# Weight conversion with both halves per instruction and an add of whole words on VectorE, bonus sums of six chunks by TensorE, and a new hand-written first order

## The chip, the cores and the metric

The kernel runs on one core of one Trainium2 chip. The metric is the device time of one execution in microseconds (us). In what follows PE is TensorE, DVE is VectorE, ACT is ScalarE, POOL is GpSimd and SP is SyncE; PEld is PE's weight load. "L156" is line 156 of the kernel before; in the changed kernel the same statements stand some lines later.

## The reference

A linear attention with a decay per channel over 768 steps, for 4 batches and 8 heads of 48 channels, then a feed-forward network (FFN) whose gate is h cos h. Everything is float32.

```python
for t in range(S):                                   # attention, S = 768
    kt, vt, rt, wt = k[:, :, t], v[:, :, t], r[:, :, t], w[:, :, t]
    cur = np.einsum('bhd,bhe->bhde', u[None] * kt, vt)
    y[:, :, t] = np.einsum('bhd,bhde->bhe', rt, state + cur)
    state = wt[:, :, :, None] * state + np.einsum('bhd,bhe->bhde', kt, vt)
x = y as (3072 tokens, 384)
h = x @ w_in                                         # 384 x 2048
out = (h * np.cos(h)) @ w_out                        # 2048 x 384
```

The term with u is the bonus of the present step: for each token and head the sum over the 48 channels of r k u, times v. The kernel calls this sum cd: 128 tokens by 8 heads.

## The kernel before

**Tiling.** The attention is cut into 24 chunks of 128 tokens (4 batches of 6 chunks), taken in the order of the list `order`, two batches side by side. The FFN takes blocks of two chunks (256 tokens). The FFN's 2048 columns are 16 tiles of 128, called f-tiles; two f-tiles make a unit, so a block has 8 units. A unit is `mm1` (18 matmuls into the tile ph, L342), then the gate on ACT, DVE and POOL (L315 to L328), then `mm2` (12 matmuls into acc, L356). Matmuls keep float32 accuracy by splitting each operand into a high part and a rest, and by three products (`PASSES`).

**Weights.** The weights come to the chip as float64 bit patterns, 64 bits a value. An f-tile has two halves ("kinds"): 384 columns of the first matrix and 384 of the second. `fetch_weights` (event `f`) loads one f-tile of raw words, 768 KB, on SP's queue. `load_weights` (event `w`) turns it into float32 and splits it: ACT scales the high word into h and takes the carry rd from the low word (L125), DVE shifts h left by 3 (L155) and puts the sign in (L156), an integer add of h and rd follows (L158, on POOL), ACT casts the high part (L130) and DVE or POOL subtracts to get the rest (L133). With `MERGE = 0` each of these instructions works on one half, 384 words; the rest of the first half is DVE's, that of the second is POOL's (`wlo0="v"`, `wlo1="p"`).

**A chunk** passes these events: `load` (r, k and w with channels on the partitions: tile tt, 674 KB), `lr` (r and k with tokens on the partitions: tile rk), `lv` (v), `decay` (two scans on DVE, L190 and L197, and the products L201 and L202), `diag` (the bonus sums cd, L206 to L209, and two diagonal fills on POOL, L213), `a` (scores pa, L233, and masked copies on DVE, L235), `t` and `s` (state), `d` (decay of the state), `y` (output, L285 and L289, a copy yf on ACT and six small DMAs into xf), `x` (split of xf into xT for the FFN). `NEEDS` and `FREES` list which event must come before which.

**What sets the order.** For the first six chunks and the first two blocks the order is written out by hand: `START` is a list of events, and `PAIR` says for each of the 16 units in it whether it belongs to block 0 or 1. PE follows this order as written. The other engines' queues are ordered by a scheduler that looks at the same events. In this first part the table `EARLY` says which engine does what (v DVE, a ACT, p POOL, s SP); after it `LATER` and the repeating `PLAN` hold, and the weights are done. `BUFS` gives the number of buffers of each tile. All loads and the DMAs into xf stand in one queue, SP's.

```python
        place = min(range(max(f + 1, NF + 1 - RING), NF + 1), key=lambda p: last.get(p, -1))
        nc.gpsimd.tensor_tensor(out=h, in0=h, in1=rd, op=ALU.add)
        nc.vector.copy_predicated(a["asb", h], mask, pa[h])
```

The first line is the place of the raw words: they lie where later weights will stand, in a ring of five. The second is the add on POOL. The third waits for the diagonal fill of the same chunk.

Of the kernel before, what the change touches and what calls it, by code (L numbers as in the profile page):

```python
# [62 lines left out]
@with_exitstack  # L63
def rwkv_cos_ffn(ctx: ExitStack, tc: tile.TileContext, tr, tn, u, wts, w, rkw, vst, us, xs, out):
    nc = tc.nc
# [76 lines left out]
    def load_weights(f):  # L142

        bits = raw.pop(f)
        wgt[f] = wt.tile([128, 2, 2, DM], F32R, tag=f"w{f}", name=f"w{f}")
        step = 2 if MERGE else 1
        for kind in range(0, 2, step):
            high, rest = wgt[f][:, kind:kind + step, 0], wgt[f][:, kind:kind + step, 1]
            words = bits[:, kind:kind + step].rearrange("p k (n w) -> p k n w", w=2)
# [5 lines left out]
            nc.vector.tensor_scalar(out=h, in0=h, scalar1=3, scalar2=None, op0=ALU.logical_shift_left)  # L155
            nc.vector.scalar_tensor_tensor(out=h, in0=hi, scalar=sign_bit, in1=h,  # L156
                                           op0=ALU.bitwise_and, op1=ALU.bitwise_or)
            nc.gpsimd.tensor_tensor(out=h, in0=h, in1=rd, op=ALU.add)  # L158
# [45 lines left out]
    def att_diag(a):  # L204
        rk = a["rk"][:, 0]
        E["rk"].tensor_tensor(out=rk, in0=rk, in1=a["rk"][:, 1], op=ALU.mult)  # L206
        E["ru"].tensor_tensor(out=rk, in0=rk, in1=u_sb, op=ALU.mult)
        cd = buf("cd", [C, 8], F32)
        nc.vector.tensor_reduce(out=cd, in_=rk.rearrange("p (h d) -> p h d", d=HD), axis=mybir.AxisListType.X, op=ALU.add)  # L209
# [403 lines left out]
```

## Time and profile before

| | us |
|---|---|
| median of 3 runs | 604.78 |
| lowest, highest | 603.35, 605.7 |
| the profiled execution | 603.12 |
| its span in the trace | 601.4 |
| PE busy in the span | 524.5 (87%) |
| DVE, ACT, POOL busy | 446.1, 245.2, 268.2 |

The page slices the span into 40 equal parts; each digit is the busy share of a slice in tenths, and in the row PEclk the clock that was granted to PE.

```profile
PE   2513744998998999999999999999999999999995
DVE  6989899998765785786696758858957865767641
ACT  2533765552333334334433353343343334334541
POOL 4675658663333543443354433434434333422231
PEclk9999858897997999999999999999999999999998
```

A slice is 15 us. The hand-written first order takes the first twelve; in the first seven of them PE has low digits and DVE high ones. From the fourteenth on PE is at 9 until the last slice.

### The profile page before, as it was taken

To read this page: it belongs to the slowest core of one execution; us is meant where nothing else is said; L and a number is where in the kernel's file an instruction comes from. 1 tells how busy PE (TensorE), PEld (TensorE's weight loads), DVE (VectorE), ACT (ScalarE), POOL (GpSimd) and SP (SyncE) were. 2 spreads that over 40 slices of the span, in tenths; PEclk is the share of its full clock that TensorE was granted. 3 is DMA by queue.
4 is the path that set the end of the run, shared out by engine and by line. 5 is a ranking of instruction groups with operands and counts; after the bars stand their busy time and mean duration, and the time that the engine had idled before them with its cause. 6 is when DMAs were issued, how large, how long until landed. Compare 5 with 4: busy or idle time off the path is not lost.

```text
span 601.4 us, 11254 instructions
## 1 busy us (share of the span) xinstructions
PE 524.5 (87%) x4372; PEld 496.4 (83%) x4372; DVE 446.1 (74%) x759; ACT 245.2 (41%) x440; POOL 268.2 (45%) x320
## 2 busy tenths in 40 slices
PE   2513744998998999999999999999999999999995
PEld 1403744887988999999999999999999999899994
DVE  6989899998765785786696758858957865767641
ACT  2533765552333334334433353343343334334541
POOL 4675658663333543443354433434434333422231
PEclk9999858897997999999999999999999999999998
DMA  8718156030342134124223121331242032055000
GB/s 267 270 66 320 47 204 191 1 106 27 99 130 78 45 99 122 44 60 126 83 74 116 54 73 53 99 101 47 79 126 65 9 100 73 2 174 187 36 1 32
DMA packets 23725, 58.47 MB, mean 97 GB/s; under 512 B 4208, under 2 KB 15088, under 8 KB 23664
## 3 DMA queue, kind: packets, MB, share of 16 engines
q1 hardware_dynamic: 23664, 57.68, 31.1%
q8 instruction: 36, 0.59, 0.4%
q14 instruction: 25, 0.20, 0.1%
HBM read 48.22 MB, written 4.72 MB: 88 GB/s over the span
## 4 chain that ended last, share of the span: by engine, by line
PE 66%; DVE 19%; DMA 6%; issue 4%; POOL 3%; ACT 1%; SPq 0%; DVEq 0%; POOLq 0%
PE ph L342 29%; PE acc L356 26%; DMA tt<-tr 6%; PE py L285 3%; PE py L289 3%; PE pa L233 3%; POOL h L158 2%; DVE h L156 2%; DVE h L155 2%; DVE shrink L193 2%; PE pst L260 2%; DVE xT L133 2%; DVE rr L320 1%; DVE w L133 1%; PE pt L242 1%
## 5 line engine op out<-in xcount | busy, mean ns | idle before, releaser
L342 PE MATMUL ph<-xT,w 128*128 128x256 f32 x1728 | 226.2, 288 | 36.3 <-DVE xT L130 31.2
L342 PEld LDWEIGHTS ph<-xT,w 128*128 128x128 f32 x1728 | 217.4, 195 | 41.7 <-DVE xT L130 29.4
L356 PE MATMUL acc<-w,gs 128*128 128x384 f32 x1152 | 218.7, 340 | 0.0
L133 POOL TENSOR_TENSOR gs<-rr,gs 128x256 fp32r<-128x256 f32 x176 | 137.7, 801 | 168.5 <-DVE gs L130 152.9
L356 PEld LDWEIGHTS acc<-w,gs 128*128 128x128 f32 x1152 | 197.8, 189 | 2.9 <-issue 0.6
L321 ACT ACTIVATE rr<-rr 128x512 f32<-128x512 f32 x96 | 60.7, 632 | 164.0 <-DVE rr L320 163.9
L319 ACT ACTIVATE rr<-ph 128x512 int32<-128x512 f32 x96 | 57.0, 594 | 102.5 <-PE ph L342 100.0
L323 DVE SCALAR_TENSOR_TENSOR rr<-rr,ph 128x512 f32<-128x512 f32 x96 | 65.4, 681 | 42.5 <-ACT rr L322 42.3
L320 DVE SCALAR_TENSOR_TENSOR rr<-rr,ph 128x512 f32<-128x512 int32 x96 | 65.0, 678 | 33.7 <-ACT rr L319 33.7
L322 ACT ACTIVATE rr<-rr 128x512 f32<-128x512 f32 x96 | 60.6, 631 | 2.5
L158 POOL TENSOR_TENSOR h<-h,rd 128x384 int32<-128x384 int32 x32 | 41.2, 1293 | 22.9 <-DVE h L156 20.1
L190 DVE TENSOR_TENSOR_SCAN ee<-tt,one_e 112x516 f32<-112x516 f32 x24 | 30.8, 1283 | 27.7 <-DMA tt<-tr 27.6
L130 DVE CAST gs<-rr 128x512 fp32r<-128x512 f32 x96 | 41.6, 433 | 6.9 <-PE acc L356 6.8
L213 POOL TENSOR_SCALAR_AFFINE_SELECT asb<-cd 128x512 f32<-128x512 f32 x48 | 32.6, 703 | 19.4 <-PE py L285 13.6
L233 PE MATMUL pa<-tt 48*128 48x128 f32 x384 | 34.1, 310 | 8.0 <-ACT kn L130 3.8
L233 PEld LDWEIGHTS pa<-tt 48*128 48x128 f32 x384 | 28.1, 208 | 14.8 <-ACT kn L130 4.3
L201 POOL TENSOR_TENSOR tt<-tt 112x512 f32<-112x512 f32 x18 | 21.5, 1193 | 35.3 <-DVE tt L197 35.3
L226 POOL TENSOR_TENSOR dd<-sn,ee 112x192 f32<-112x192 f32 x16 | 9.6, 601 | 61.9 <-DVE ee L190 52.1
L130 ACT CAST w<-h 128x384 fp32r<-128x384 f32 x32 | 16.4, 512 | 47.9 <-POOL h L158 47.8
L235 DVE COPY_PREDICATED asb<-mask,pa 128x512 f32<-128x512 uint8 x48 | 32.5, 725 | 0.0
L285 PE MATMUL py<-asb,v 128*48 128x128 f32 (+1 forms) x384 | 30.1, 294 | 1.1 <-DVE asb L235 1.1
L197 DVE TENSOR_TENSOR_SCAN tt<-tt,inj 112x516 f32<-112x516 f32 x24 | 30.8, 1285 | 0.2
(61 smaller groups left out, 428.9 us busy)
## 6 DMA issues: line engine op xcount, KB each, us to landing
tt<-tr SPq DMA_DIRECT2D x24, 674.2 KB, 5.3
raw<-wts SPq DMA_DIRECT2D x16, 768.0 KB, 8.1
rk<-tn SPq DMA_DIRECT2D x24, 384.0 KB, 3.5
v<-tn SPq DMA_DIRECT2D x24, 192.0 KB, 2.4
out<-ob SPq DMA_DIRECT2D x24, 192.0 KB, 2.1
ww<-w SPq DMA_DIRECT2D x6, 768.0 KB, 4.5
xf<-yf SPq DMA_DIRECT2D x48, 72.0 KB, 3.3
xf<-yf SPq DMA_DIRECT2D x48, 16.0 KB, 2.8
```

The source lines that it names most:

```text
L130: (nc.scalar.copy if E[name] is nc.scalar else E[name].tensor_copy)(out=out, in_=in_)
L133: E[name].tensor_tensor(out=out, in0=full, in1=high.bitcast(F32), op=ALU.subtract)
L158: nc.gpsimd.tensor_tensor(out=h, in0=h, in1=rd, op=ALU.add)
L233: nc.tensor.matmul(out=pa[h][:, p], lhsT=a["k3"][rows(h), p], rhs=a["r3"][rows(h), p], start=True, stop=True)
L285: nc.tensor.matmul(out=py[ROW * h:ROW * h + m, p], lhsT=a["v"][:, head_cols(p, h)], rhs=a["asb", h][:, p], start=p == 0, stop=not past, sk ...
L319: nc.scalar.activation(nn, ph, AF.Copy, scale=INV2PI / W_SCALE)
L320: nc.vector.scalar_tensor_tensor(out=rr, in0=nn, scalar=-2.0 * math.pi * W_SCALE, in1=ph, op0=ALU.mult, op1=ALU.add)
L321: nc.scalar.activation(rr, rr, AF.Sin, scale=0.5 / W_SCALE)
L322: nc.scalar.activation(rr, rr, AF.Square)
L323: nc.vector.scalar_tensor_tensor(out=rr, in0=rr, scalar=-0.5, in1=ph, op0=ALU.add, op1=ALU.mult)
L342: nc.tensor.matmul(out=ph[:, fi], lhsT=wgt[u * FU + fi][:, 0, a, kt * 128:(kt + 1) * 128], rhs=xT[:, b, kt], start=n == 0, stop=n == 3 * K ...
L356: nc.tensor.matmul(out=accs[i][j][:, :DM], lhsT=gs[:, a, fi, j * C:(j + 1) * C], rhs=wgt[u * FU + fi][:, 1, b], start=u == 0 and fi == 0 a ...
```

## The change

- **Both halves per instruction.** `MERGE = 1`: every instruction of `load_weights` takes 768 words in place of 384, half as many instructions. The buffers follow: h from 6 of 384 words to 2 of 768, rd from 3 to 1.
- **The add on DVE.** `wadd="v"`: the integer add of h and rd is DVE's, not POOL's. Since the second half has no instruction of its own any more, `wlo1="p"` is without effect and the whole rest (768) is DVE's too. POOL has no part in the conversion any more. (A second way of setting the sign is in the code, with the tiles sign and three; with `wsg="v"` it isn't used.)
- **Bonus sums by PE for chunks 0 to 5** (`BY_PE = 6`). `decay` begins with a product rkt = r k on DVE, channels on the partitions; four small matmuls against u laid out by head (`u_by_head`, a new load of 112x8 values) sum it into pc, and ACT copies pc to cd. These six chunks load no rk; the load of u_sb moves behind the load of chunk 6.
- **Buffers:** tt 2 to 3, v 2 to 4.
- **A new `START` and `PAIR`.** `lr0` to `lr5` are gone, the units and the conversions stand otherwise to each other. Before, the 16 conversions were done ahead of the 14th `mm1`; now the last two stand between the 14th and the 15th.

```diff
-MERGE = 0
-BUFS = dict(tt=2, rk=2, v=2, h=6, rd=3, rr=7, ... cd=1)
+MERGE = 1
+BUFS = dict(tt=3, rk=2, v=4, h=2, rd=1, sign=1, rr=7, ... cd=1, rkt=1)
...
+         "y2 f w f load4 y3 s3 f w t3 mm1 mm2 mm2 decay4 w load5 mm1 load6 w mm1 decay5 diag4 lv4 lr6 f f t4",
...
-PAIR = "0000110111110001"
+PAIR = "0000111011101001"
@@ load_weights
-            scaled("wm", h.bitcast(F32), hi.bitcast(F32), 2.0 ** -111)
+            nc.scalar.activation(h.bitcast(F32), hi.bitcast(F32), AF.Copy, scale=2.0 ** -111)
             rd = buf("rd", [128, step, DM], I32)
-            scaled("rd%d" % kind, rd, lo.bitcast(U32), 2.0 ** -29)
+            nc.scalar.activation(rd, lo.bitcast(U32), AF.Copy, scale=2.0 ** -29)
...
-            nc.gpsimd.tensor_tensor(out=h, in0=h, in1=rd, op=ALU.add)
+            E["wadd"].tensor_tensor(out=h, in0=h, in1=rd, op=ALU.add)
@@ att_load
+        if j == 0:
+            E["qt"].dma_start(out=u_by_head, in_=ut)
+        if j == BY_PE:
+            E["qt"].dma_start(out=u_sb, in_=u.to_broadcast([C, DM]))
@@ att_decay
+        if a["j"] < BY_PE:
+            a["rkt"] = buf("rkt", [R, NP, C], F32)
+            E["rkt"].tensor_tensor(out=a["rkt"], in0=a["r3"], in1=a["k3"], op=ALU.mult)
@@ att_diag
+        if a["j"] < BY_PE:
+            pc = bank("a", [C, 512], "pc")[:, :8]
+            for p in range(NP):
+                nc.tensor.matmul(out=pc[:, 2 * p:2 * p + 2], lhsT=a["rkt"][:, p], rhs=u_by_head[:, p], start=True, stop=True)
+            cd = buf("cd", [C, 8], F32)
+            copy("cd", cd, pc)
+        else:
...
```

What this does to the queues is seen at three places. **DVE, the first f-tile and the second chunk's scans, before** (w_161 is the first f-tile):

```order
L156 SCALAR_TENSOR_TENSOR h<-raw,sign_bit,h 128x384
L190 SCALAR_TENSOR_TENSOR ee<-tt,one_e 112x516
L155 TENSOR_SCALAR h<-h 128x384
L193 TENSOR_TENSOR shrink<-shrink,ee 112x4
L195 TENSOR_SCALAR whole<-ee 112x4
L156 SCALAR_TENSOR_TENSOR h<-raw,sign_bit,h 128x384
L196 RECIPROCAL inj<-whole 112x4
L235 COPY_PREDICATED asb<-mask,pa 128x512
L197 SCALAR_TENSOR_TENSOR tt<-tt,inj 112x516
L235 COPY_PREDICATED asb<-mask,pa 128x512
L201 TENSOR_TENSOR tt<-tt 112x512
L133 TENSOR_TENSOR w_161<-h,w_161 128x384
```

and now, where the first f-tile is called w_178 (the row ISA is the integer add, over 1536 elements of 16 bits):

```order
L160 SCALAR_TENSOR_TENSOR h<-raw,sign_bit,h 128x768
L201 TENSOR_TENSOR rkt<-tt 112x512
L204 SCALAR_TENSOR_TENSOR ee<-tt,one_e 112x516
L167 ISA h<-h,rd 128x1536
L207 TENSOR_TENSOR shrink<-shrink,ee 112x4
L209 TENSOR_SCALAR whole<-ee 112x4
L210 RECIPROCAL inj<-whole 112x4
L211 SCALAR_TENSOR_TENSOR tt<-tt,inj 112x516
L256 COPY_PREDICATED asb<-mask,pa 128x512
L215 TENSOR_TENSOR tt<-tt 112x512
L256 COPY_PREDICATED asb<-mask,pa 128x512
L136 TENSOR_TENSOR w_178<-h,w_178 128x2x384
```

The add and the whole rest of the tile have come to DVE, in place of two instructions per step there is one, and the product rkt stands ahead of the scan.

**ACT, from the second chunk's kn to its output copy yf, before** (w_296 and w_379 are the third and fourth f-tile):

```order
L130 COPY kn<-pt 128x384
L125 ACTIVATE h<-raw 128x384
L130 CAST w_296<-h 128x384
L125 ACTIVATE rd<-raw 128x384
L125 ACTIVATE h<-raw 128x384
L130 CAST w_296<-h 128x384
L125 ACTIVATE rd<-raw 128x384
L125 ACTIVATE h<-raw 128x384
L130 CAST w_379<-h 128x384
L125 ACTIVATE rd<-raw 128x384
L130 CAST w_379<-h 128x384
L130 COPY yf<-py 112x512
```

and now (w_314 is the third f-tile):

```order
L133 COPY kn<-pt 128x384
L155 ACTIVATE h<-raw 128x768
L133 CAST w_314<-h 128x2x384
L133 COPY yf<-py 112x512
L157 ACTIVATE rd<-raw 128x768
L155 ACTIVATE h<-raw 128x768
L133 CAST w_324<-h 128x2x384
```

The copy yf of chunk 1 stood behind both casts of the fourth f-tile; now it stands behind the third's, and the rd of the next f-tile comes after the cast of this one.

**POOL, from the first diagonal fill, before:**

```order
L213 AFFINE_SELECT asb<-cd 128x512 x2
L158 TENSOR_TENSOR h<-h,rd 128x384
L202 TENSOR_TENSOR tt<-tt,ee 112x512
L158 TENSOR_TENSOR h<-h,rd 128x384
L133 TENSOR_TENSOR w_161<-h,w_161 128x384
L158 TENSOR_TENSOR h<-h,rd 128x384
L213 AFFINE_SELECT asb<-cd 128x512 x2
```

and now:

```order
L234 AFFINE_SELECT asb<-cd 128x512 x3
L216 TENSOR_TENSOR tt<-tt,ee 112x512
L234 AFFINE_SELECT asb<-cd 128x512 x2
L216 TENSOR_TENSOR tt<-tt,ee 112x512
L234 AFFINE_SELECT asb<-cd 128x512
L216 TENSOR_TENSOR tt<-tt,ee 112x512
L136 TENSOR_TENSOR gs<-rr,gs 128x256
```

Between the fills and the products of the decay nothing is left of the conversion.

More of the change, by code (lines that the diff above doesn't have):

```diff
@@ L27 @@
 BLK = 2
+BY_PE = 6
 BT = BLK * C
@@ L31 @@
 BY_HAND = "P"
-MERGE = 0
-BUFS = dict(tt=2, rk=2, v=2, h=6, rd=3, rr=7, gs=2, asb=4, ahl=2, sn=2, yf=1, past=2, xT=2, kn=2, ee=2, dd=2, xf=6, cd=1)
+MERGE = 1
+BUFS = dict(tt=3, rk=2, v=4, h=2, rd=1, sign=1, rr=7, gs=2, asb=4, ahl=2, sn=2, yf=1, past=2, xT=2, kn=2, ee=2, dd=2, xf=6, cd=1, rkt=1)
 LEAST = 1e-15
@@ L63, in rwkv_cos_ffn @@
 @with_exitstack
-def rwkv_cos_ffn(ctx: ExitStack, tc: tile.TileContext, tr, tn, u, wts, w, rkw, vst, us, xs, out):
+def rwkv_cos_ffn(ctx: ExitStack, tc: tile.TileContext, tr, tn, u, ut, wts, w, rkw, vst, us, xs, out):
     nc = tc.nc
@@ L107, in rwkv_cos_ffn @@
     u_sb = cst.tile([C, DM], F32, name="u_sb")
+    u_by_head = cst.tile([R, NP, 2], F32, name="u_by_head")
     shrink = cst.tile([R, NP], F32, name="shrink")
@@ L115, in rwkv_cos_ffn @@
     nc.vector.memset(sign_bit, -(1 << 31))
+    three = cst.tile([128, 1], I32, name="three")
+    nc.vector.memset(three, 3)
     raw, wgt, last = {}, {}, {}
@@ L151, in load_weights @@
             h = buf("h", [128, step, DM], I32)
-            scaled("wm", h.bitcast(F32), hi.bitcast(F32), 2.0 ** -111)
+            nc.scalar.activation(h.bitcast(F32), hi.bitcast(F32), AF.Copy, scale=2.0 ** -111)
             rd = buf("rd", [128, step, DM], I32)
-            scaled("rd%d" % kind, rd, lo.bitcast(U32), 2.0 ** -29)
[L155 to L158, printed above, removed]
+            nc.scalar.activation(rd, lo.bitcast(U32), AF.Copy, scale=2.0 ** -29)
+            if E["wsg"] is nc.vector:
+                nc.vector.tensor_scalar(out=h, in0=h, scalar1=3, scalar2=None, op0=ALU.logical_shift_left)
+                nc.vector.scalar_tensor_tensor(out=h, in0=hi, scalar=sign_bit, in1=h,
+                                               op0=ALU.bitwise_and, op1=ALU.bitwise_or)
+            else:
+                sign = buf("sign", [128, step, DM], I32)
+                nc.gpsimd.tensor_scalar(out=sign, in0=hi, scalar1=-(1 << 31), scalar2=None, op0=ALU.bitwise_and)
+                nc.vector.scalar_tensor_tensor(out=h, in0=h, scalar=three, in1=sign,
+                                               op0=ALU.logical_shift_left, op1=ALU.bitwise_or)
+            E["wadd"].tensor_tensor(out=h, in0=h, in1=rd, op=ALU.add)
             hf = h.bitcast(F32)
@@ L178, in att_load_rk @@
         E["qr"].dma_start(out=rk, in_=tn[a["g"], :, 0:2])
-        if a["j"] == 0:
-            E["qr"].dma_start(out=u_sb, in_=u.to_broadcast([C, DM]))
     def att_load_v(a):
@@ L204, in att_diag @@
     def att_diag(a):
[L205 to L209, printed above, removed]
+        if a["j"] < BY_PE:
[4 more added lines that the diff above has]
+            copy("cd", cd, pc)
+        else:
+            rk = a["rk"][:, 0]
+            E["rk"].tensor_tensor(out=rk, in0=rk, in1=a["rk"][:, 1], op=ALU.mult)
+            E["ru"].tensor_tensor(out=rk, in0=rk, in1=u_sb, op=ALU.mult)
+            cd = buf("cd", [C, 8], F32)
+            nc.vector.tensor_reduce(out=cd, in_=rk.rearrange("p (h d) -> p h d", d=HD), axis=mybir.AxisListType.X, op=ALU.add)
         for h in range(2):
@@ L386, in att @@
             return
-        for m in NEEDS.get(n, "").split():
+        for m in ("decay" if n == "diag" and j < BY_PE else NEEDS.get(n, "")).split():
             att(j, m)
@@ L592, in slay @@
         return x.reshape(B, NP, 2, S, D).transpose(3, 2, 4, 0, 1).reshape(S, 2 * D, B * NP)
+    ut = np.zeros((2, ROW, NP, 2), np.float32)
+    for h in range(2):
+        ut[h, :D, :, h] = u.reshape(NP, 2, D)[:, h].T
     us = np.broadcast_to(u.reshape(NP, 2, D).transpose(1, 2, 0).reshape(2 * D, 1, NP), (2 * D, B, NP))
```

5 lines of the change are left out of this document (3 added, 2 removed), and 8 rows, old and new, of the table START.

## Prediction

> **What bounds the kernel now.** I read first the busy time by stage, cut where the program changes: the first FFN matmul (53.5 us), the last FFN matmul of the hand-written first order (177.4), the tail (570, left out here). Columns: window, length, then busy time and count of PE, PEld, DVE, ACT, POOL, granted clock, DMA share, GB/s.
>
> ```profile
> 0.00:53.50 53.50, 13.55 (x104) 10.80 (x104) 45.17 (x76) 19.50 (x40) 31.39 (x33) 1.00 0.63 208
> 53.50:177.40 123.90, 98.69 (x754) 92.72 (x755) 107.77 (x182) 62.04 (x121) 67.87 (x63) 0.86 0.35 115
> 177.40:570.00 392.60, 388.13 (x3352) 369.06 (x3351) 283.93 (x486) 154.13 (x264) 160.28 (x213) 0.99 0.28 83
> ```
>
> From 177.4 us on PE is busy 388.1 of 392.6 us and the change leaves that code alone. PE stands idle 40.0 + 25.2 = 65.2 us in the first order; that is the only place where this change can win or lose. There DVE is busy 45.2 + 107.8 = 152.9 of 177.4 us, the most of the four engines that feed PE. So the first order is set by the length of DVE's queue and by its idle 24.5 us, and the rest of the program follows its end one for one.
>
> Next, what DVE does in 0 to 177.4 us (groups by line and shape: total us, mean ns of one):
>
> ```profile
> L156 DVE SCALAR_TENSOR_TENSOR h<-raw,sign_bit,h 128x384 int32<-128x384 int32 x32 | 26.4, 832 | 0.1
> L155 DVE TENSOR_SCALAR h<-h 128x384 int32<-128x384 int32 x32 | 17.9, 581 | 0.8 <-ACT h L125 0.8
> L133 DVE TENSOR_TENSOR w<-h,w 128x384 fp32r<-128x384 f32 x16 | 10.9, 687 | 4.6 <-ACT w L130 4.6
> L190 DVE TENSOR_TENSOR_SCAN ee<-tt,one_e 112x516 f32<-112x516 f32 x8 | 10.9, 1360 | 8.2 <-DMA tt<-tr 8.1
> L133 DVE TENSOR_TENSOR gs<-rr,gs 128x256 fp32r<-128x256 f32 x16 | 9.8, 614 | 0.1
> L130 DVE CAST gs<-rr 128x512 fp32r<-128x512 f32 x16 | 8.4, 522 | 1.1 <-PE acc L356 1.1
> L207 DVE TENSOR_TENSOR rk<-rk,u_sb 128x384 f32<-128x384 f32 x10 | 6.3, 628 | 0.0
> L206 DVE TENSOR_TENSOR rk<-rk 128x384 f32<-128x384 f32 x10 | 6.0, 605 | 0.0
> L133 DVE TENSOR_TENSOR xT<-xf,xT 128x384 fp32r<-128x384 f32 x5 | 6.0, 1191 | 0.0
> L209 DVE TENSOR_REDUCE cd<-rk 128x8 f32<-128x384 f32 x9 | 4.9, 544 | 1.6 <-POOL asb L213 1.6
> L193 DVE TENSOR_TENSOR shrink<-shrink,ee 112x4 f32<-112x4 f32 x7 | 4.5, 643 | 0.1
> L226 DVE TENSOR_TENSOR dd<-sn,ee 112x192 f32<-112x192 f32 x4 | 4.0, 1002 | 0.0
> L158 POOL TENSOR_TENSOR h<-h,rd 128x384 int32<-128x384 int32 x32 | 41.2, 1293 | 22.9 <-DVE h L156 20.1 <-ACT w L130 1.1 <-ACT rr L321 1.1
> L133 POOL TENSOR_TENSOR w<-h,w 128x384 fp32r<-128x384 f32 x16 | 18.9, 1184 | 7.5 <-ACT w L130 7.5
> ```
>
> A multiply of 4 elements (L193) that takes 643 ns on average is the thing to notice. The timeline shows why, and gives each form's undisturbed time:
>
> ```profile
> 5.55 1.23 DVE L190 TENSOR_TENSOR_SCAN ee<-tt,one_e 112x516 f32<-112x516 f32 x1 [3.48 <-DMA tt<-tr]
> 22.26 0.34 DVE L155 TENSOR_SCALAR h<-h 128x384 int32<-128x384 int32 x1
> 28.19 0.61 DVE L156 SCALAR_TENSOR_TENSOR h<-raw,sign_bit,h 128x384 int32<-128x384 int32 x1
> 32.23 1.18 POOL L202 TENSOR_TENSOR tt<-tt,ee 112x512 f32<-112x512 f32 x1 [1.49 <-PE py L285]
> 32.26 1.16 DVE L193 TENSOR_TENSOR shrink<-shrink,ee 112x4 f32<-112x4 f32 x1
> 33.42 0.55 DVE L133 TENSOR_TENSOR w<-h,w 128x384 fp32r<-128x384 f32 x1
> 34.63 3.56 POOL L158 TENSOR_TENSOR h<-h,rd 128x384 int32<-128x384 int32 x1 [1.23 <-DVE h L156]
> 36.13 0.68 DVE L201 TENSOR_TENSOR tt<-tt 112x512 f32<-112x512 f32 x1
> 63.56 0.42 DVE L130 CAST gs<-rr 128x512 fp32r<-128x512 f32 x1
> 173.71 0.42 DVE L133 TENSOR_TENSOR gs<-rr,gs 128x256 fp32r<-128x256 f32 x1
> 178.12 0.17 DVE L193 TENSOR_TENSOR shrink<-shrink,ee 112x4 f32<-112x4 f32 x1
> ```
>
> The L193 at 32.26 us ran until a POOL instruction that began 0.03 us before it was over (1.16 against 1.18 us); the one at 178.12 took 0.17. And a POOL add beside a busy DVE took 3.56 us. **DVE and POOL hold each other up**, so work taken from POOL is partly won on DVE.
>
> **The change part by part.**
>
> *Weights, both halves per instruction.* On DVE today: 26.4 + 17.9 + 10.9 = 55.2 us. At the undisturbed times it would be 32 x 0.61 + 32 x 0.34 + 16 x 0.55 = 39.2, so 16.0 us are waits for POOL. Afterwards a tile is four instructions over 768 words. From 0.55 us (384, two inputs) and 0.68 (512, two inputs) 384 words more cost 0.39: low part 0.94, sign 1.00; the shift, 0.34 with one input, gets half of that, 0.53. The add is new on DVE and the trace of before has none like it. The order shows it as one instruction over 1536 16-bit elements. By bytes it is a two-input instruction over 768 words, 0.94 us; by elements it is 0.55 + 1152 x 0.13/128 = 1.72. I take 0.94, because the two-input rows differ by the bytes they carry, and keep 1.72 for the range. Sum 3.41 x 16 = 54.6 us undisturbed, as much as the disturbed 55.2 of today although DVE takes over 32 adds and 16 low parts.
>
> [...]
>
> *POOL.* It loses L158 and its half of the low parts, 41.2 + 18.9 = 60.1 of the 31.4 + 67.9 = 99.3 us in the first order; 0.39 is left. I scale the waits on DVE by that. Of the weights' 16.0 us 6.3 stay: weights 54.6 + 6.3 = 60.9, **+5.7 us**. In the other rows the waits are: gs (614 - 420) x 16 = 3.1, xT (1191 - 550) x 5 = 3.2, L193 (643 - 170) x 7 = 3.3, the gate's casts (522 - 420) x 16 = 1.6, L190 (1360 - 1230) x 8 = 1.0, and L226, half as long as a 0.55 us row, at least (1002 - 550) x 4 = 1.8. Of these 14.0 us 0.61 goes: **-8.5 us**.
>
> *Bonus sums by PE.* Six chunks lose L206, L207, L209: 6 x (0.605 + 0.628 + 0.544) = 10.7 us, and gain a product of 112x512 (L201's form, 0.68): 4.1. **-6.6 us**. For the 24 small matmuls there are two rows of PE:
>
> ```profile
> 29.14 0.98 PE L260 MATMUL pst<-v,kn 128*64 128x48 f32 x15 [0.87 <-ACT kn L130]
> L242 PE MATMUL pt<-ident,tt 112*128 112x112 f32 x26 | 5.0, 327 | 12.5 <-POOL tt L202 8.1 <-DVE asb L235 4.4
> ```
>
> They cost PE between 24 x 0.98/15 = 1.6 us (the state matmuls' pace) and 24 x 0.327 = 7.8 (a transpose each); I take 2, the nearer in size, and count nothing, for they lie in PE's 65 us of idle time; without that cover they would be the 2. The six cd copies go to ACT, busy 81.5 of 177.4 us; each is a new wait, for behind a late copy stand the two diagonal fills on POOL, then the masked copies on DVE and the output matmuls on PE. POOL's queue, freed of the conversion, leaves them room, so I count nothing; a whole ACT cast late each time it would be 6 x 0.76 = 4.6.
>
> *Idle time of DVE.* The row that matters is on the way to the first FFN matmul:
>
> ```profile
> ACT w L130 <- POOL h L158: 47.8, 27, 6.1
> ACT h L125 <- DMA raw<-wts: 8.7, 1, 8.7
> 38.23 0.51 ACT L130 CAST w<-h 128x384 fp32r<-128x384 f32 x1 [6.06 <-POOL h L158]
> 42.18 0.58 ACT L130 COPY yf<-py 112x512 f32<-112x512 f32 x1
> 53.57 0.58 PE L342 MATMUL ph<-xT,w 128*128 128x256 f32 x1 [21.60 <-DVE xT L130]
> ```
>
> PE had finished chunk 1's output at 53.57 - 21.60 = 32.0 us, but its copy (42.18) stood on ACT behind a cast that waited 6.06 us for the slow POOL add; 11.4 us after the copy PE could start. Now that copy stands behind the third tile's cast, which follows the third add on DVE. By the order and the times above DVE's rows up to that add come to 24 us; with 3.5 us until the first chunk lands, some 5 us of waits and ACT's cast and copy it is at about 35 us instead of 42. And the first raw weights (ACT waited 8.7 us) have no rk and no u_sb in front of them on SP; six rk loads go, u_sb moves behind the load of chunk 6, and a load of 3.6 KB comes. I expect the first FFN matmul some 7 us earlier, and of the 20 us of DVE's idle time after the first chunk's arrival 4 us gone; bounds 12 gone and, with shallower h and rd buffers, 28 more (below). **-4 us**.
>
> *New first order, PAIR, tt and v buffers.* The order moves weights 15 and 16 behind more FFN units and puts chunk 1's product ahead of chunk 0's scores on PE, so these wait for the second tt load. DVE's queue is no shorter for that: 0, bounds as for the idle time. After the first order nothing is left to win, as the third stretch of the first view shows.
>
> Sum: 5.7 - 8.5 - 6.6 - 4 = **-13.4 us**. The profiled run took 603.1 us (its span 601.4 and 1.7 around it), so 589.7; the median of the runs, 604.8, lies 1.7 us above that run and gives 591.4. I say 591.
>
> **The rivals.**
>
> *PE becomes the bound of the first order (more gained).* If the chains shorten more, 12 instead of 4 us of DVE's idle time go: 583; if the waits for POOL go altogether too (6.3 us and 5.5 that I left standing), 572. For it: ACT's 47.8 us behind POOL vanish. Against: DVE's own rows stay, and PE needs its 16 + 16 units after its first FFN matmul whatever comes, which is 67 us by the chain in order of time (18 matmuls 2.12 us, 12 matmuls 2.09):
>
> ```profile
> 215.53 2.12 PE ph L342 x18
> 217.65 2.09 PE acc L356 x12
> ```
>
> Chance 0.2, around 581.
>
> *The add runs an element a tick.* 16 x (1.72 - 0.94) = 12.5 us more on DVE: 604, no measurable change. For it: no row shows two inputs at two elements a tick. Chance 0.12.
>
> *One rd buffer makes a ring (slower).* Before, rd had three buffers and h six halves; now ACT may write the next tile's rd only after DVE's add has read this one, and in ACT's queue that stands behind this tile's cast. Cast and rd have the rows
>
> ```profile
> L125 ACT ACTIVATE rd<-raw 128x384 int32<-128x384 uint32 x32 | 17.4, 545 | 0.0
> L321 ACT ACTIVATE rr<-rr 128x512 f32<-128x512 f32 x16 | 10.1, 629 | 15.5 <-DVE rr L320 15.4
> ```
>
> so 128 words more cost ACT 0.084 us; over 768 words the cast (0.51 at 384) takes 0.76 and rd 0.80, and with hand-overs the ring is some 1.75 us. If DVE sits through that on every tile it loses 16 x 1.75 = 28 us: 619. It makes the kernel slower from (13.4 + 3) / 16 = 1.0 us a tile. Behind a waiting add on DVE stand the gates, and PE waits for those. Against: between two adds the new order has three or more other instructions on DVE, at least 2.5 us at the times above, so most is covered. Chance 0.1.
>
> *The gain is lost at the hand-over.* The first order ends earlier, but chunk 5's output still goes by DMA to xT before block 2 can start, where PE waited 2.81 us,
>
> ```profile
> 181.81 1.46 PE L342 MATMUL ph<-xT,w 128*128 128x256 f32 x3 [2.81 <-DVE xT L130]
> ```
>
> and DVE has the decay work of chunks 6 and 7, which didn't get shorter, in the way. Half the gain: 598. Chance 0.08.
>
> **How the numbers follow.** Forecast 591 with chance 0.5 (own range 584 to 597); more gained 0.2; add an element a tick 0.12; lost at the hand-over 0.08; ring 0.1. Under 0.5% (3 us) a measurement cannot tell a change from none, so faster is below 601.8 us: 0.5 + 0.2 + 0.08 = 0.78; same 0.12; slower 0.1. The range leaves out the ring and the lower half of the case with more gained: 579 to 604.
>
> **What would show it.** The add's row on DVE near 0.94 us, or 1.7. L193's mean well under 0.643, POOL's busy time near 40 us in the first order. First FFN matmul near 46 us, last of the first order near 164. DVE's idle time in front of the add with ACT rd as its releaser under 1 us a tile. If DVE's busy share in the first order falls under 0.8 while PE still waits there, my bound is wrong; so it is if POOL's instructions grow no shorter and DVE's mean times stay.

## The result, and the profile after

The changed kernel took 578.27 us (median; 577.43 to 580.27), the kernel before on the same chip 604.23 (603.35 to 605.7): a ratio of 0.9573, 95% interval 0.9539 to 0.9607. It is faster, as forecast, but by 26 us where 13.4 were forecast; the time lies 0.7 us below the range. The profiled execution after took 577.43 us, its span 575.7, so 25.7 us of span are to be explained.

The slices of the page (40 equal parts, now 14.4 us each):

```profile
PE   1736799989899999999999999999999999999995
...
DVE  6999899999997866866957675775676575684431
...
POOL 2222134335446445334545444543553443223231
PEclk9976889989999999999999999999999999999998
```

DVE now has a 9 or an 8 in every slice from the second to the twelfth, POOL starts at 2 where it had 4 to 8, and PE reaches 9 in the sixth slice and keeps to 8 or 9 from there until the last one.

Busy time by stage after, cut at the same places of the program as in the prediction (first FFN matmul, last FFN matmul of the first order, tail left out); columns: window, length, busy time and count of PE, PEld, DVE, ACT, POOL, granted clock, DMA share, GB/s:

```profile
0.00:42.20 42.20, 18.26 (x128) 15.95 (x128) 35.48 (x60) 15.65 (x23) 10.83 (x17) 0.93 0.62 193
42.20:155.40 113.20, 99.28 (x779) 93.19 (x780) 108.71 (x177) 61.52 (x97) 40.15 (x33) 0.89 0.39 133
155.40:544.30 388.90, 387.06 (x3349) 369.11 (x3348) 270.85 (x480) 153.97 (x264) 168.06 (x210) 1.00 0.28 83
```

The first stage went from 53.5 to 42.2 us, the second from 123.9 to 113.2, and the rest of the span from 424.0 (601.4 - 177.4) to 420.3 (575.7 - 155.4). So 11.3, 10.7 and 3.7 us were won in the three. What DVE did in the first order: busy 45.2 + 107.8 = 152.9 us before, 35.5 + 108.7 = 144.2 after, which is 8.8 less; idle (length less busy) 8.3 + 16.1 = 24.5 before, 6.7 + 4.5 = 11.2 after, which is 13.3 less. **More was won by DVE standing idle less than by DVE having less to do.**

The groups of instructions after, 0 to 155.4 us, for the rows that the prediction priced (busy us in total, mean ns of one | idle before and its releaser):

```profile
L136 POOL TENSOR_TENSOR gs<-rr,gs 128x256 fp32r<-128x256 f32 x16 | 24.0, 1497 | 44.4 <-DVE gs L133 44.4
L160 DVE SCALAR_TENSOR_TENSOR h<-raw,sign_bit,h 128x768 int32<-128x768 int32 x16 | 16.7, 1041 | 0.1
L136 DVE TENSOR_TENSOR w<-h,w 128x768 fp32r<-128x768 f32 x16 | 15.1, 944 | 0.0
L167 DVE CUSTOM_DVE_ANT_0 h<-h,rd 128x1536 uint16<-128x1536 uint16 x16 | 15.1, 943 | 0.0
...
L211 DVE TENSOR_TENSOR_SCAN tt<-tt,inj 112x516 f32<-112x516 f32 x8 | 11.2, 1396 | 0.1
...
L136 DVE TENSOR_TENSOR gs<-rr,gs 128x256 fp32r<-128x256 f32 x16 | 9.8, 610 | 0.0
L159 DVE TENSOR_SCALAR h<-h 128x768 int32<-128x768 int32 x16 | 8.9, 562 | 1.1 <-ACT h L155 1.1
...
L222 PE MATMUL pc<-u_by_head,rkt 112*128 112x2 f32 x48 | 8.4, 297 | 13.1 <-DVE rkt L201 13.1
...
L133 DVE CAST gs<-rr 128x512 fp32r<-128x512 f32 x16 | 7.1, 444 | 1.3 <-PE acc L377 1.3
...
L201 DVE TENSOR_TENSOR rkt<-tt 112x512 f32<-112x512 f32 x6 | 4.5, 756 | 4.0 <-DMA tt<-tr 4.0
L207 DVE TENSOR_TENSOR shrink<-shrink,ee 112x4 f32<-112x4 f32 x8 | 4.3, 536 | 0.0
...
L136 DVE TENSOR_TENSOR xT<-xf,xT 128x384 fp32r<-128x384 f32 x5 | 2.7, 547 | 0.0
...
L247 DVE TENSOR_TENSOR dd<-sn,ee 112x192 f32<-112x192 f32 x4 | 1.4, 338 | 0.0
```

The add takes 943 ns for 768 words. The split of xT (1191 ns before) and dd (1002) came down to 547 and 338, but DVE's gs (614 before) is still at 610, and POOL's gs has risen from 1076 ns to 1497.

What engines waited for in the first order, before (DVE's rows; columns: who <- for whom: us in total, times, longest):

```profile
DVE ee L190 <- DMA tt<-tr: 8.1, 3, 3.5
DVE w L133 <- ACT w L130: 4.6, 4, 2.7
DVE rr L320 <- ACT rr L319: 3.5, 2, 2.0
DVE rr L323 <- ACT rr L322: 2.1, 2, 1.4
```

and after (DVE's largest, its largest for ACT, and ACT's wait ahead of its cast, which was 47.8 us for POOL's add before):

```profile
ACT w L133 <- DVE h L167: 11.7, 7, 3.1
...
DVE rkt L201 <- DMA tt<-tr: 4.0, 2, 3.4
...
DVE h L159 <- ACT h L155: 1.1, 1, 1.1
```

Before, 10.2 us of DVE's idle time lay in front of instructions that waited for ACT (4.6, 3.5, 2.1), and 8.1 in front of scans that waited for a load. After, the one such row for ACT among the larger ones is 1.1 us, and the loads' is 4.0.

### The profile page after: what moved, and what is told of

It reads as the page before. It is cut to its first block, busy times and chain, and to the rows that moved or that the text cites. A ratio compares the mean times of both kernels' runs of the same rounds, so it can differ in the third digit from the quotient of the medians.

```text
span 575.7 us, 11220 instructions
## 1 busy us (share of the span) xinstructions
PE 529.5 (92%) x4420; PEld 502.8 (87%) x4420; DVE 424.7 (74%) x732; ACT 240.7 (42%) x398; POOL 227.6 (40%) x272
## 4 chain that ended last, share of the span: by engine, by line
PE 70%; DVE 15%; DMA 7%; issue 3%; ACT 3%; SPq 1%; POOL 0%; DVEq 0%; ACTq 0%; POOLq 0%
PE acc L377 29%; PE ph L363 27%; PE py L306 4%; PE pa L254 4%; DMA tt<-tr 3%; DMA ww<-w 3%; PE py L310 3%; PE pst L281 2%; DVE rr L341 2%; PE pt L263 1%; DVE tt L211 1%; DVE h L167 1%; DVE rr L344 1%; DVE ee L204 1%; DVE h L160 1%
## 5 line engine op out<-in xcount | busy, mean ns | idle before, releaser
L136 POOL TENSOR_TENSOR gs<-rr,gs 128x256 fp32r<-128x256 f32 x176 | 155.6, 903 | 257.7 <-DVE gs L133 194.9
L363 PE MATMUL ph<-xT,w 128*128 128x256 f32 x1728 | 222.5, 285 | 12.9 <-DVE xT L133 9.5
L363 PEld LDWEIGHTS ph<-xT,w 128*128 128x128 f32 x1728 | 215.2, 191 | 16.2 <-DVE xT L133 9.8
L344 DVE SCALAR_TENSOR_TENSOR rr<-rr,ph 128x512 f32<-128x512 f32 x96 | 65.4, 681 | 36.4 <-ACT rr L343 35.5
L234 POOL TENSOR_SCALAR_AFFINE_SELECT asb<-cd 128x512 f32<-128x512 f32 x48 | 33.2, 712 | 26.7 <-ACT cd L133 26.6
L204 DVE TENSOR_TENSOR_SCAN ee<-tt,one_e 112x516 f32<-112x516 f32 x24 | 29.8, 1243 | 17.2 <-DMA tt<-tr 17.2
L211 DVE TENSOR_TENSOR_SCAN tt<-tt,inj 112x516 f32<-112x516 f32 x24 | 34.1, 1423 | 0.2
L254 PE MATMUL pa<-tt 48*128 48x128 f32 x384 | 31.8, 298 | 2.3 <-ACT cd L133 2.2
L254 PEld LDWEIGHTS pa<-tt 48*128 48x128 f32 x384 | 26.4, 198 | 8.2 <-issue 3.9
L215 POOL TENSOR_TENSOR tt<-tt 112x512 f32<-112x512 f32 x18 | 21.6, 1201 | 27.4 <-DVE tt L211 27.4
L306 PEld LDWEIGHTS py<-asb,v 128*64 128x64 f32 (+1 forms) x384 | 24.8, 143 | 1.6 <-issue 0.8
L133 ACT COPY yf<-py 112x512 f32<-112x512 f32 x24 | 13.9, 581 | 20.6 <-PE py L310 20.3
L310 PE MATMUL py<-tt,dd 48*48 48x128 f32 x320 | 22.5, 281 | 0.0
```

Of the source, the lines that this page charges most:

```text
L133: (nc.scalar.copy if E[name] is nc.scalar else E[name].tensor_copy)(out=out, in_=in_)
L136: E[name].tensor_tensor(out=out, in0=full, in1=high.bitcast(F32), op=ALU.subtract)
L211: nc.vector.tensor_tensor_scan(out=wp[:, 0:W129], data0=wp[:, 0:W129], data1=inj.rearrange("p a t -> p (a t)"), initial=0.0, op0=ALU.mult, ...
L254: nc.tensor.matmul(out=pa[h][:, p], lhsT=a["k3"][rows(h), p], rhs=a["r3"][rows(h), p], start=True, stop=True)
L306: nc.tensor.matmul(out=py[ROW * h:ROW * h + m, p], lhsT=a["v"][:, head_cols(p, h)], rhs=a["asb", h][:, p], start=p == 0, stop=not past, sk ...
L344: nc.vector.scalar_tensor_tensor(out=rr, in0=rr, scalar=-0.5, in1=ph, op0=ALU.add, op1=ALU.mult)
```

## The experiments

All times are medians; each ratio stands beside the kernel before as run on the same chip. "First stage" is the time of the first FFN matmul, "end" that of the last FFN matmul of the first order, "rest" the span from there. The table is worked out from the traces as above; "busy" and "idle" are DVE's up to the end. The letters in the expectations stand for the theories that they name.

| kernel | us | ratio, 95% interval | first stage | end | busy | idle | rest |
|---|---|---|---|---|---|---|---|
| before | 604.23 | | 53.6 | 177.4 | 152.9 | 24.5 | 424.0 |
| after | 578.27 | 0.9573 (0.9539 to 0.9607) | 42.3 | 155.4 | 144.1 | 11.2 | 420.4 |
| m1: add and second rest on DVE, halves apart | 589.12 | 0.9778 (0.9742 to 0.9813) | 43.5 | 167.4 | 155.1 | 12.3 | 421.0 |
| m2: halves together, add on POOL | 595.0 | 0.9876 (0.983 to 0.9923) | 49.1 | 168.5 | 151.8 | 16.7 | 424.8 |
| a1: both, nothing else of the change | 584.9 | 0.9705 (0.9663 to 0.9746) | 43.2 | 155.9 | 145.3 | 10.6 | 426.2 |
| a2: new order alone | 603.1 | 1.0 (0.998 to 1.002) | 54.1 | 176.6 | 157.8 | 18.8 | 423.7 |
| a4: a1 and the tt and v buffers | 583.2 | 0.9669 (0.9629 to 0.9709) | 45.2 | 162.1 | 150.2 | 11.9 | 419.6 |
| u1: change with the add on POOL | 596.93 | 0.9889 (0.9836 to 0.9942) | 49.2 | 171.1 | 147.8 | 23.2 | 423.3 |
| u2: change without bonus by PE | 591.88 | 0.9787 (0.973 to 0.9844) | 46.5 | 169.9 | 150.3 | 19.6 | 420.7 |
| u3: change with 2 tt, 2 v buffers | 583.66 | 0.9663 (0.9613 to 0.9713) | 42.3 | 156.7 | 143.6 | 13.1 | 426.8 |
| u4: change with the old order | 583.02 | 0.9667 (0.9615 to 0.9719) | 41.7 | 157.7 | 145.8 | 11.9 | 421.6 |

**Add back on POOL (u1).** The changed kernel, with the conversion's add of 768 words on POOL.

```diff
-EARLY = dict(rkt="v", cd="a", wsg="v", wadd="v", ...
+EARLY = dict(rkt="v", cd="a", wsg="v", wadd="p", ...
```

> The changed kernel with the integer add of the weights given back to POOL (768 words in one instruction), all else as changed. Theory A (the idle time of DVE went because ACT's casts no longer stand behind POOL's adds, and DVE's own rows wait less for POOL): DVE loses 15 us of adds but gets waits back, the cast w on ACT waits for POOL again by 20 us or more in total, DVE idle in the first order rises from 11 us to 18 or more; time 583 to 592. Rival B (the third tt buffer and the new order took the idle time away, the add's place doesn't matter): DVE is 15 us shorter and its idle time stays near 11; time 566 to 576.

It took 596.93 us, slower than either expectation: this one letter gives back 18.7 of the 26 us (596.93 - 578.27). Stages of u1, and its add in the groups:

```profile
0.00:49.20 49.20, 18.56 (x128) 16.00 (x128) 41.42 (x58) 17.89 (x25) 20.59 (x23) 0.93 0.59 192
49.20:171.10 121.90, 101.43 (x778) 94.21 (x779) 106.44 (x165) 58.93 (x94) 59.52 (x44) 0.89 0.37 118
```

```profile
L167 POOL TENSOR_TENSOR h<-h,rd 128x768 int32<-128x768 int32 x16 | 36.5, 2282 | 44.9 <-DVE h L160 34.2 <-ACT rd L157 3.6 <-ACT h L155 3.0
```

DVE lost the 15.1 us of its 16 adds, but its busy time rose by 3.7 (144.1 to 147.8): beside POOL its other steps took longer (the sign 1281 ns instead of 1041), and a ninth first scan lies ahead of the end. Its idle time more than doubled, 11.2 to 23.2. POOL itself is busy for only 80 of 171 us: it isn't short of time, it is late. It waits 34.2 us in all for DVE's sign, each add then takes 2.28 us, and ACT's cast waits for it:

```profile
ACT w L133 <- POOL h L167: 37.8, 16, 7.4
```

**Add and second rest on DVE, halves apart (m1).** The kernel before, with the add and the second half's rest on DVE; halves, buffers, order and bonus as before.

```diff
-            nc.gpsimd.tensor_tensor(out=h, in0=h, in1=rd, op=ALU.add)
+            nc.vector.tensor_tensor(out=h, in0=h, in1=rd, op=ALU.add)
...
-wlo0="v", wlo1="p"
+wlo0="v", wlo1="v"
```

> The kernel before with the adds and the second half's rest on DVE, but one half per instruction as before (h of 6, rd of 3 buffers, two tt). Theory A (POOL out of the conversion is what counts, the merging saves fixed costs only): 32 instructions of each kind cost DVE 32 x 4 x some 0.07 us less 16 x 4 x 0.07, so 4 to 5 us more than the weights' part alone at 584.9: 587 to 592. Rival M (merging is the larger part): 597 to 604.

It took 589.12 us, as my theory had it. But no row shows the theory's 0.07 us an instruction: the weights' rows come to 68.4 us in m1 (the three below and 13.0 for the shift) and to 55.4 in a1, so the 64 instructions more cost 13.0 us, 0.2 each with their waits for POOL, where 4 to 5 us were expected; the time is 4.2 us above that of a1 (589.12 - 584.9). Stages of m1, three of its four rows of the weights on DVE (sign, rest, add), and ACT's wait:

```profile
0.00:43.50 43.50, 13.36 (x104) 10.76 (x104) 38.20 (x79) 17.68 (x36) 10.88 (x17) 0.89 0.75 245
43.50:167.40 123.90, 100.85 (x754) 94.40 (x755) 116.91 (x232) 64.02 (x125) 38.84 (x34) 0.83 0.35 119
```

```profile
L156 DVE SCALAR_TENSOR_TENSOR h<-raw,sign_bit,h 128x384 int32<-128x384 int32 x32 | 20.0, 630 | 0.0
L133 DVE TENSOR_TENSOR w<-h,w 128x384 fp32r<-128x384 f32 x32 | 17.9, 566 | 3.1 <-ACT w L130 3.1
L158 DVE CUSTOM_DVE_ANT_0 h<-h,rd 128x768 uint16<-128x768 uint16 x32 | 17.5, 545 | 0.0
```

```profile
ACT w L130 <- DVE h L158: 31.1, 16, 6.3
```

DVE has 2.2 us *more* to do than before (38.2 + 116.9 = 155.1 against 152.9), and the first order still ends 10 us earlier, since its idle time is 5.3 + 7.0 = 12.3 instead of 24.5. The 2.2 us are a balance: DVE took on 17.5 us of adds and 7.0 more of rests (10.9 to 17.9), and all its other rows together gave back 22.3, the sign alone 6.4 (832 to 630 ns each), which fits a POOL that holds them up less (busy 49.7 us instead of 99.3). So what was won has two parts: less time lost inside DVE's instructions, and less between them. ACT still waits 31.1 us for the add; but now it waits for an engine that is busy with its own queue meanwhile.

**Halves together, add on POOL (m2).** The kernel before with `MERGE = 1`, h=2, rd=1.

```diff
-MERGE = 0
-BUFS = dict(tt=2, rk=2, v=2, h=6, rd=3, ...
+MERGE = 1
+BUFS = dict(tt=2, rk=2, v=2, h=2, rd=1, ...
```

> The kernel before with both halves per instruction (h of 2, rd of 1 buffer, the whole rest on DVE) and the add left on POOL over 768 words. Theory A: ACT's casts still stand behind POOL's adds, now twice as long, 598 to 608. Rival M (merging is the larger part): 586 to 594.

It took 595.0 us, between the two expectations: 7.2 us less than before (602.16 on its chip), where m1 gave 13.0 and a1 (below) gives 18.6. The second half's rest has left POOL in all three, so its share is in both single gains, and 7.2 and 13.0 can't be put down to the halves and to the add alone. POOL's conversion is 31.7 us in m2 instead of 60.1 (41.2 + 18.9). The second stage of m2, for the comparison with a1, which differs from it by the add alone (some 10 us, 595.0 to 584.9):

```profile
49.10:168.50 119.40, 98.02 (x755) 90.66 (x756) 108.63 (x163) 59.32 (x91) 55.46 (x42) 0.91 0.34 112
```

**The weights' part alone (a1)** is m2 with the add on DVE:

```diff
-            nc.gpsimd.tensor_tensor(out=h, in0=h, in1=rd, op=ALU.add)
+            nc.vector.tensor_tensor(out=h, in0=h, in1=rd, op=ALU.add)
```

> The kernel before with the weights' part alone: both halves per instruction, the add and the whole rest on DVE, h of 2 and rd of 1 buffer; bonus sums, buffers and order as before. Theory A (taking POOL out of the conversion is the larger part): DVE's weight rows stay near 55 us, its other rows lose 8 to 10 us of waits and its idle time 5 to 9, 586 to 592. Rival C (the new order was needed for it): 598 to 604.

It took 584.9 us, 18.6 less than before on its chip (603.48), and a little less than either expectation. Its stages:

```profile
0.00:43.10 43.10, 12.48 (x104) 10.26 (x104) 36.90 (x65) 15.85 (x20) 12.28 (x16) 1.00 0.79 261
43.10:155.90 112.80, 95.45 (x755) 88.48 (x756) 108.37 (x177) 60.59 (x93) 34.94 (x32) 0.95 0.38 123
```

Its first order ends at 155.9, where that of the whole change ends at 155.4. All that the first order won is there without the bonus sums, the order or the buffers. What a1 lacks lies in the rest, 426.2 against 420.4.

**The new order alone (a2).** The kernel before with the new `START` and `PAIR`.

```diff
... (START likewise)
-PAIR = "0000110111110001"
+PAIR = "0000111011101001"
```

> The kernel before with the new first order and pairing alone. Theory A: the order by itself does little, 600 to 608. Rival C: it takes 8 us or more of idle time away, 590 to 596.

603.1 us, ratio 1.0 (0.998 to 1.002): no difference, as expected. Idle time fell by 5.7 us and busy time rose by 4.9.

**The old order in the changed kernel (u4)**, without the loads `lr0` to `lr5`:

```diff
... (START likewise)
-PAIR = "0000111011101001"
+PAIR = "0000110111110001"
```

> The changed kernel with the first order and the unit pairing of before (without the rk loads of chunks 0 to 5), all else as changed. Theory A: DVE's work is the same and the order only shifts idle time a little, 578 to 583. Rival C (the new order took the idle time away): DVE idle in the first order goes from 11 back towards 20 us or more, 586 to 592.

583.02 us, 4.7 slower than the change and at the upper edge of the first expectation. The order that is worth nothing alone is worth something beside the other parts.

**Two tt and two v buffers in the changed kernel (u3).**

```diff
-BUFS = dict(tt=3, rk=2, v=4, ...
+BUFS = dict(tt=2, rk=2, v=2, ...
```

> The changed kernel with two tt and two v buffers as before, all else as changed. Theory A: the chunk loads had 4 us of DVE's waits before, so at most 4 us come back, 578 to 582. Rival B (the third tt buffer is what took the idle time away): DVE's wait for tt loads goes from 4.3 back to 8 us or more and chains behind it too, 584 to 590.

583.66 us, 5.4 slower and short of the second expectation. Its first order ends 1.3 us later than that of the change; the rest is where it loses, 426.8 against 420.4. The stretch behind the first order of u3, to set beside the third row of after (155.40 to 544.30):

```profile
156.70:552.10 395.40, 388.34 (x3350) 368.01 (x3349) 283.23 (x484) 154.00 (x264) 160.07 (x213) 1.00 0.29 83
```

PE is idle for 395.40 - 388.34 = 7.06 us of it, in the change for 388.90 - 387.06 = 1.84, in the kernel before for 392.60 - 388.13 = 4.47. What PE waits for there in u3:

```profile
PE ph L363 <- DVE xT L136: 4.2, 7, 0.8
PE ph L363 <- DVE xT L133: 2.6, 3, 1.8
```

ten waits for the next block's xT; in the change there is one, of 0.3 us.

**The weights' part with the buffers (a4)**: a1 with the line of u3 the other way round.

```diff
-BUFS = dict(tt=2, rk=2, v=2, h=2, rd=1, ...
+BUFS = dict(tt=3, rk=2, v=4, h=2, rd=1, ...
```

> The weights' part alone on the kernel before (584.9 us), with three tt and four v buffers added. Theory A (the third tt buffer is worth 5 to 6 us behind the first order: in the runs with two, 426 to 427 us follow its end, with three 420 to 422): 579 to 581. Rival D (that stretch is short in the changed kernel because the bonus sums and the order leave DVE free at the hand-over): 584 to 586.

583.2 us (before on its chip 602.16), between the two; against a1 (ratio 0.9669 to 0.9705) that is no difference that the intervals separate. The rest fell from 426.2 to 419.6, as between u3 and the change. But the first order ended 6.2 us later. The first FFN matmul is 2.0 us later already, and the scans wait 5.4 us for loads instead of 4.0; then, with a third buffer, the decay work of the next chunks comes earlier (the first order of a4 holds nine of each of DVE's two scans, that of a1 seven; DVE's busy time 145.3 to 150.2), and DVE is the busiest engine there. By these counts the third buffer moves DVE's work out of the rest and into the first order; I take it that it pays where the first order can take it.

**Bonus sums on DVE again (u2).** `BY_PE = 0` in the changed kernel. With its tables the product with u goes to POOL, and the rk loads stand directly at the bonus step, so it is not a pure undoing.

```diff
-BY_PE = 6
+BY_PE = 0
```

> The changed kernel with the bonus sums of all chunks on DVE again (no rkt, no pc), all else as changed. Theory A (DVE's rows set the first order): DVE gets 6.6 us more and six rk loads come back in front of weights, so 585 to 590. Rival B (hidden, PE sets the first order by now): within 2 us of the changed kernel, 577 to 580.

591.88 us, slower than expected, and slower than a1, which has the bonus on DVE as well. DVE's busy time is 6.2 us longer than in the change, close to the price of that part (6.6), but not for that reason. With the product on POOL, DVE's own bonus rows come to 11.6 us (4.8 + 2.5 + 4.3), against 11.3 in the change (6.8, and rkt 4.5). It is the weights' rows that grew, from 55.8 to 61.3 us, beside a busier POOL (57.8 us against 51.0); the sign, at 1041 ns in the change:

```profile
L160 DVE SCALAR_TENSOR_TENSOR h<-raw,sign_bit,h 128x768 int32<-128x768 int32 x16 | 19.7, 1231 | 0.1
```

DVE's idle time is 8.4 us longer, with 5.9 us in front of a gate step that waits for ACT. So the run shows that this arrangement loses 13.6 us; that the new order needs the bonus sums on PE it doesn't show, since the product on POOL and the late rk loads came with it.

**Three attempts to win more from the changed kernel.** DVE's casts of gs and xT on ACT (n1), one of the two products behind the decay, L215, on POOL (n5), bonus sums of chunks 6 and 7 by PE too (n2):

```diff
-gh="v", yf="a", xh="v"
+gh="a", yf="a", xh="a"
```

> The changed kernel with the casts of the gate's high part and of xT in the first order on ACT instead of DVE. If DVE's rows still set the first order, DVE is 9 us shorter (casts of 0.425 and 0.54 us, 16 and 5 of them) and ACT, busy half of the time, takes them: 570 to 575. If PE's queue or the chains of one unit set it, the longer chain through ACT (two more hand-overs per gate) shows: 578 to 584.

```diff
-r3="v"
+r3="p"
```

> The changed kernel with the product r3 of the decay of chunks 0 to 5 on POOL instead of DVE (708 ns each on DVE). If DVE's rows set the first order and POOL, busy 51 of 155 us, has the room: DVE 4.3 us shorter, 574 to 577, a version faster than both. If POOL's slower product (1.2 us and more) stands in a chain that PE waits for (it comes before the scores), the saving is given back as idle time: 578 to 583.

```diff
-BY_PE = 6
+BY_PE = 8
... (rkt and cd in LATER, no lr6 in START)
```

> The changed kernel with the bonus sums of chunks 6 and 7 by PE too, without the rk loads of these two. If DVE's work on chunks 6 and 7 at the hand-over still holds PE up: 575 to 577. If not, PE has eight small matmuls more and nothing else changes: 578 to 580.

581.54 us (0.9621, 0.9571 to 0.9671), 580.52 (0.9651, 0.9595 to 0.9706) and 582.08 (0.9653, 0.9609 to 0.9697): none beats the change, and of each the slower expectation came, or a time beyond it. n1 goes the other way from m1: it takes work off DVE and puts ACT into its chains. Its trace is of an execution of 587.12 us, 5.6 above the median, so its waits may be larger than in most; its stages, and DVE's waits for ACT:

```profile
0.00:45.30 45.30, 18.46 (x128) 15.97 (x128) 38.45 (x63) 17.67 (x27) 12.63 (x18) 1.00 0.70 216
45.30:161.60 116.30, 103.22 (x778) 96.72 (x779) 102.10 (x156) 70.05 (x115) 34.87 (x32) 0.90 0.37 121
```

```profile
DVE gs L136 <- ACT gs L133: 4.0, 4, 1.5
...
DVE rr L341 <- ACT rr L340: 3.2, 2, 2.4
...
DVE rr L344 <- ACT rr L343: 1.8, 2, 1.1
```

DVE has 3.6 us less to do (38.5 + 102.1 = 140.5) and 9.9 us more idle time (6.9 + 14.2 = 21.1 against 11.2), 9.0 of it in front of steps that now wait for ACT. In n5 six products left DVE, and its busy time stayed at 144.0: beside a busier POOL (58.8 us against 51.0) the weights' rows grew from 55.8 to 58.7 us and the split of gs from 9.8 to 11.6, and a ninth first scan came ahead of the end. In n2 the first order ended 1.0 us later and the rest took 424.0.

## Why the prediction was right, and where it was wrong

**DVE bounds the first order: right by its share (152.9 of 177.4 us busy before, 144.2 of 155.4 after), but its queue's length was half of the story.** I had the end of the first order as DVE's work plus its idle time, and came close with the work. m1 shows that the two move apart: more work, 10 us less time.

**DVE's work: -9.4 forecast, -8.8 measured, with errors that cancel, so that the nearness of the sum is luck.** The *weights* were to cost +5.7; by the groups they cost 16.7 + 15.1 + 15.1 + 8.9 = 55.8 against 55.2, +0.6. The undisturbed price of 54.6 was close, the add's 0.94 right to the last digit; but of the 6.3 us of waits for POOL that I left standing, 1.2 are left. The *other rows' waits* were to fall by 8.5 and fell by 8.4, though not as scaled: by the groups' totals xT 6.0 to 2.7, dd 4.0 to 1.4, the gate's casts 8.4 to 7.1, the first scan 10.9 to 9.9, L193's form 4.5 to 4.3 (it still takes 536 ns), and gs nothing (9.8 both times). The *bonus* was to give 6.6 and gave 5.9: L206, L207 and L209 (17.2 us before) are 6.8 now, and rkt is 4.5, at 756 ns each instead of 680. What I had not counted: with the third tt buffer more of chunk 7's decay lies ahead of the end. There are eight second scans (L211, 11.2 us) where seven stood (9.0) and stand in u3, which has two buffers; with the small steps and a product behind them it is some 4 us.

**DVE's idle time, "-4 us": the step that failed.** It fell by 13.3 us. I read the cause rightly, ACT's casts behind POOL's slow add, and followed it only along the way to the first FFN matmul. There the copy yf was to go at about 35 us and the matmul 7 us earlier:

```profile
35.21 0.58 ACT L133 COPY yf<-py 112x512 f32<-112x512 f32 x1
```

```profile
42.29 0.58 PE L363 MATMUL ph<-xT,w 128*128 128x256 f32 x1 [9.04 <-DVE xT L133]
```

The copy went at 35.21 instead of 42.18, as forecast, and the matmul at 42.29, 11.3 us earlier: from copy to matmul it was 11.4 us and is now 7.1. In between, the last DMA of the copy into xf was issued at 45.88 us before and at 38.92 after, and DVE's cast of xT began at 52.97 and at 41.69; DVE wasn't idle ahead of either, so these 4.3 us, which I had not counted, passed in DVE's queue. The earlier landing of the raw words, which I had counted, isn't needed for it: a1 has the old loads, ACT waits 10.7 us for the words there (1.7 in the change), and its first FFN matmul is at 43.2 us.

But DVE's idle time in this stage fell by only 1.6 (8.3 to 6.7); its work fell by 9.7. The rest of the idle time, 16.1 to 4.5 us, went **after** the first FFN matmul, where the other conversions run among the gates, and for that stage I had written no term. By the waits in that stage, DVE's idle time for ACT went from 7.5 us (3.5 + 2.1 + 1.9) to 1.1 and that for chunk loads from 4.6 to 0.9. Two pairs of kernels differ by the place of the add alone: 15.5 us idle in that stage with the add on POOL (u1) against 4.5 (after), and 10.8 (m2) against 4.4 (a1). So it is shown both in the old order and in the new one that the place of the add counts. It doesn't count alone: with the add on POOL the halves together took the 16.1 to 10.8 (m2) and the new order to 10.4 (a2), and with the add on DVE it is 7.0 in m1, 11.9 in u2 and 14.2 in n1.

How the add does it is read from the waits, not shown by a run of its own: in a chain DVE, POOL, ACT, DVE for each tile, with ACT's gate steps queued behind the waiting cast, DVE runs dry; in a chain DVE, ACT, DVE it does not. No run separated ACT's queue from POOL's slowness.

**"After the first order nothing is left to win": the second step that failed.** The rest fell by 3.7 us. One part is the hand-over, one of the rivals: I feared a loss there of half the gain, and it was a gain. The 11 us behind the first order's end, before, after and in u3 (the clock is the third number from the end):

```profile
177.40:188.40 11.00, 7.99 (x49) 7.33 (x48) 7.76 (x14) 1.84 (x4) 2.68 (x3) 0.69 0.29 92
```

```profile
155.40:166.40 11.00, 10.51 (x120) 9.44 (x119) 9.16 (x16) 2.98 (x6) 2.62 (x3) 1.00 0.69 202
```

```profile
156.70:167.70 11.00, 8.77 (x85) 8.07 (x85) 7.29 (x14) 3.00 (x6) 2.50 (x3) 0.84 0.36 116
```

PE did 120 matmuls where it had done 49. The wait for chunk 5's xT is down from 2.81 us to 0.27:

```profile
157.25 3.03 PE L363 MATMUL ph<-xT,w 128*128 128x256 f32 x20 [0.27 <-DVE xT L133]
```

I took PE's 388.1 busy of 392.6 us as full. The missing 4.5 us were nearly all waits for xT (2.8 and 1.5), and the granted clock was 0.99 over the stretch, 0.69 in its first 11 us. The buffers of tt and v, which I had priced at nothing, remove such waits (no run parts the two): 7.06 us of idle time in u3, 1.84 in the change; 6.92 in a1 (394.80 - 387.88), 0.34 in a4 (388.20 - 387.86). They are not the whole of it: m1 has two of each, and still PE is busy for 10.33 us of the 11 behind its first order, and its rest is 421.0 us. What makes the hand-over smooth in one kernel and not in another stays open.

**The rivals.** *PE becomes the bound / more gained* (583, or 572 without any waits for POOL): the time, 578.27, fell between these two, and its condition, 12 us of DVE's idle time gone, came true with 13.3; but PE did not become the bound: in the second stage DVE is busy for 108.7 of 113.2 us and PE for 99.3. *An element a tick* fell: the add took 943 ns for 1536 elements of 16 bits, the rest (L136) 944 for 768 of fp32, and 1.72 us were estimated for this case. *The ring* fell: the wait ahead of DVE's add for rd doesn't appear, and the wait of DVE for ACT's h is 1.1 us in all. *The 24 small matmuls* (bounds 1.6 and 7.8, 2 taken) cost PE 8.4 us, just outside; I still take them as hidden, as 155.4 - 117.5 = 37.9 us of PE's time are idle there, but no run shows it. *The six cd copies*, counted as nothing, had POOL's fills wait 26.6 us, but DVE's masked copies waited only 0.5 us for these fills. *POOL near 40 us* was 10.8 + 40.2 = 51.0, mostly since its own instructions grew longer (gs alone 17.2 to 24.0 us).

**What stays open.** The way from a1 (18.6 us won) to the whole change (26.0 on its own chip) isn't the sum of its parts. Any one of order, buffers or bonus taken out of the change costs 4.7, 5.4 or 13.6 us (the last with its product on POOL); the buffers alone on top of a1 move the time by less than the intervals, and the order alone on top of the kernel before by nothing. So they depend on each other. By the counts of instructions the buffer moves decay work into the first order and the bonus by PE takes work out of DVE's queue there; that the order decides where both land is my reading. No run gives each its own share.

## What to carry to other kernels

For the engine that bounds a stage, read its idle time beside its busy time, and ask of each idle stretch which other engine's hand-over ended it; moving work *onto* the bounding engine can pay when it takes a hand-over through a slow engine out of a chain that comes back, and when that engine also held up the bounding one's own instructions (m1: 2.2 us more work, 10 us less time). Moving work off it can fail for the same two reasons: new hand-overs (n1: 3.6 us less work, 9.9 us more idle time), longer instructions beside a busier helper (n5: six products less, DVE busy for 144.0 us against 144.2). Follow such a chain through all its repetitions, not only to the first event that it delays. A stretch in which the bounding engine is busy for 99% can still hold one per cent of small waits (PE before: 4.47 us of 392.60, at a granted clock of 0.99), and more buffers can remove them (PE idle for 6.92 us in a1, for 0.34 in a4).
